# Pooled attention with a token mixer: dividing by the row sums when a batch is loaded, not per head pair

## The chip, the cores and the metric

The kernel runs on one core of one Trainium2 chip. A core has five engines with instruction queues of their own: TensorE (PE, with its weight loads shown apart as PEld), VectorE (DVE), ScalarE (ACT), GpSimd (POOL) and SyncE (SP), whose queue issues nearly all DMAs here. The metric is the device time of one execution in microseconds (us).

## The reference, cut to what matters

```python
# attention: q, k, v are (8 batches, 8 heads, 1152, 64); two neighbouring rows of q are averaged
scores = scale * np.matmul(q_pool, k.transpose(0, 1, 3, 2))          # (8, 8, 576, 1152)
scores = scores - np.max(scores, axis=-1, keepdims=True)
attn = np.exp(scores)
attn = attn / (np.sum(attn, axis=-1, keepdims=True) + 1e-09)
x = np.matmul(attn, v)                                               # heads side by side: (8, 576, 512)
# token mixer
theta = x @ w_theta
zr, zi = x * np.cos(theta), x * np.sin(theta)
u = x + w_tok_r @ zr + w_tok_i @ zi                                  # over tokens, per batch
out = u + np.maximum(u @ w_ch, 0.0)
```

The four weight matrices arrive as 64-bit floats, as pairs of 32-bit words, and are turned into 32-bit floats on the chip.

## The kernel before, in words

There are two phases. The attention phase runs over 32 pairs of heads (`i`, four pairs to a batch). The token phase runs over 8 batches (`b`).

**Order.** Every piece of work is registered with a position (`at` in the first phase, `at2` in the second), the list is sorted, and each engine then executes its own instructions strictly in that order. A pair is 18 positions long (two halves `u` of the query rows, nine key tiles `kt` each). The tables at the head of the file (`PLAN`, `W_AT`, `MAX_AT`, `TOK_AT` and so on) hold the positions. An instruction that waits holds up everything behind it on its engine, and on SP a DMA that waits holds up every later DMA.

**One pair.** `prep_t`, `prep_hi` and `prep_lo` transpose keys and queries on PE, round them on ACT (`hi`) and take the remainder on DVE (`lo`). `maxpass` and `max_tail` find row maxima: PE writes scores to PSUM, DVE reduces them (`mx`, lines 287, 306 and 307). `escore` computes each score tile with eight matmuls and ACT takes the exponential (`pc`, line 349). `ssum` adds the exponentials on POOL (`ss`, line 358). `av` multiplies them with the values (line 367) into `xu`. `norm_sum` finishes the row sums on PE and ACT adds epsilon (`sm`). PSUM is cut into four slots, used in turn by all of these. Twice in a pair, at positions 10.35 and 19.27, a `burst` stands: the transposes for a later pair, the rounding, and an `av`. In the second burst (`tail_prep`) DVE reads the slots with `mx` L306 and L307, ACT then writes `hi`, DVE writes `lo`, and only then can PE use the slot again. In the first one ACT's small copies (`tail`, then `mT` of L319) stand behind DVE's `lo`, and PE's `norm_sum` stands behind `mT`.

**Division before.** For each pair the four rows of sums go to DRAM (`norm_spread`), come back spread over 128 partitions (`norm_load`), are inverted on DVE (`norm_recip`, 128x9), go to DRAM again (`norm_save`), come back copied to 64 partitions each (`norm_bcast`, two DMAs), and DVE multiplies the pair's output by them (`norm_out`, L429, 128x576). `norm_store` then writes the pair to `xd[b]`.

**Weights.** A generator (`weights`) makes 18 jobs of some fifteen steps; nine steps stand in each pair, at the positions `W_AT`: four just ahead of the first burst, three just ahead of the second. A job fetches a slab (`raw`, one buffer), and `narrow` makes 32-bit floats with six operations on DVE (L500, L503, L505, L507, L511, L515), one on ACT (L502) and two on POOL.

**Token phase.** `xload` brings a batch into `xT` (two buffers), `xhi` (ACT) and `xlo` split it, `theta` multiplies (PE), `chain` makes sine and cosine and the products in eight steps on ACT, DVE and, last, POOL (`zlo`, L771), `token_mix` and `channel` multiply. `xlo` runs on DVE for batch 0 and on POOL for the others (L704). Batch 0 is loaded while the last pairs of the first phase still run.

Of the kernel before, what the change touches and what calls it, by code (L numbers as in the profile page):

```python
# [9 lines left out]
F32 = mybir.dt.float32  # L10
# [27 lines left out]
    "norm_spread": 29.0,  # L38
    "norm_load": 29.426,
    "norm_recip": 37.5,  # L40
    "norm_save": 37.6,
    "norm_bcast": 37.7,
    "norm_out": 46.5,
    "norm_store": 46.6,
}
# [6 lines left out]
CYC = 56  # L52
PLAN2 = {'wload': 12.0, 'xload': -64.6, 'xhi': -51.7, 'uadd0': 15.0, 'uadd1': 31.4}
THETA_AT = (-42.4, -33.8, -25.1, -15.4, -9.2)
THETA0_AT = (-70, -60, -50, -40, -30)
CHAIN0_AT = (0.5, 2, 4, 8, 13, 18, 26, 28)
X0_AT = 563
X1_AT = -4
CHAIN_AT = (4.4, 2.4, 6.3, 5.7, 10.3, 8.7, 2.8, 4.5)
# [19 lines left out]
def pooled_attention_moe_kernel(  # L79
# [48 lines left out]
    wcd = [dram.tile([ND, P, DM], F32, name=f"wcd{i}") for i in range(2)]  # L128
    xd = [dram.tile([DM, SQ], F32, name=f"xd{b}") for b in range(B)]

    def bank(kind, name):
# [22 lines left out]
    xTs = []  # L154

    def xload(b):
        xT = xTs[b % 2]
        bst[b] = {"xT": xT}
        xv = xd[b].rearrange("(c p) s -> p c s", p=P)
        nc.sync.dma_start(xT[:, :, 0:SQ], xv)  # L160
        nc.sync.dma_start(xT[:, :, SQ : 5 * P], xv[:, :, 4 * P : SQ])

    with ExitStack() as p1:
# [196 lines left out]
        def av(i, u):  # L360
            st = state[i]
            if u == 0:
                st["xu"] = nrm.tile([P, 2, HALF], F32, tag="xu", name=f"xu{i}", bufs=3)
            pa = bank2("e", f"pa{i}_{u}")
            for kt in range(KT):
                for h, hs in enumerate(HEADS):
                    nc.tensor.matmul(  # L367
                        pa[hs, 0, 0:HALF],
                        st["vn"][:, h, kt, :],
                        st["pc"][u, kt][:, h, :],  # L370
                        start=(kt == 0),
                        stop=(kt == KT - 1),
                    )
            nc.scalar.copy(st["xu"][:, u, :], pa[:, 0, 0:HALF])
# [19 lines left out]
        def norm_spread(i):  # L394
            st = state[i]
            rdi = st["rd"] = dram.tile([4, HALF], F32, tag="rd", name=f"rd{i}", bufs=2)
            nc.sync.dma_start(rdi, st["sm"].rearrange("(n r) c -> n r c", r=32)[:, 0, :])

        def norm_load(i):
            st = state[i]  # L400
            rc = st["rc"] = sml.tile([P, SQ * 2 // P], F32, tag="rc", name=f"rc{i}")
            rdv = st["rd"].rearrange("n c -> (n c)").rearrange("(p j) -> p j", p=P)
            nc.sync.dma_start(rc, rdv)

        def norm_recip(i):
            rc = state[i]["rc"]
            nc.vector.reciprocal(rc, rc)

        def norm_save(i):
            st = state[i]  # L410
            rdo = st["ro"] = dram.tile([4, HALF], F32, tag="ro", name=f"ro{i}", bufs=2)
            nc.sync.dma_start(
                rdo.rearrange("n c -> (n c)").rearrange("(p j) -> p j", p=P), st["rc"]
            )

        def norm_bcast(i):
            st = state[i]
            dn = st["dn"] = nrm.tile([P, 2, HALF], F32, tag="dn", name=f"dn{i}")
            for h in range(2):
                nc.sync.dma_start(  # L420
                    dn[h * D : (h + 1) * D].rearrange("a u c -> a (u c)"),
                    st["ro"].rearrange("(h u) c -> h (u c)", h=2)[h : h + 1, :].broadcast_to(
                        [D, SQ]
                    ),
                )

        def norm_out(i):
            st = state[i]
            nc.vector.tensor_tensor(st["xu"], st["xu"], st["dn"], ALU.mult)  # L429

# [32 lines left out]
        def norm_store(i):  # L463
# [4 lines left out]
            )  # L468
            del state[i]

        def weights():
# [17 lines left out]
            def narrow(raw, ws, R, n, g):  # L489
# [9 lines left out]
                mk = ws[0:R, 0:n]  # L499
                nc.vector.tensor_scalar(lo, lo, 8, None, ALU.logical_shift_right)  # L500
                yield
                nc.scalar.activation(tl, lo, AF.Copy, scale=2.0**-44)  # L502
                nc.vector.tensor_scalar(f, hi, 0x7FFFFFFF, None, ALU.bitwise_and)  # L503
                yield
                nc.vector.tensor_scalar(mk, f.bitcast(F32), TINY, None, ALU.max)  # L505
                yield
# [114 lines left out]
        def plan(i):  # L621
# [24 lines left out]
            for n, fn in (  # L646
                ("norm_spread", norm_spread),
                ("norm_load", norm_load),
                ("norm_recip", norm_recip),
                ("norm_save", norm_save),  # L650
                ("norm_bcast", norm_bcast),
                ("norm_out", norm_out),
                ("norm_store", norm_store),
# [6 lines left out]
        pw = ExitStack()  # L660
        wgen = weights()
        at(X0_AT, 11, early)
        for i in range(NPAIR):
            for pos in W_FIRST if i == 0 else W_AT if i < W_END else W_LAST:
# [4 lines left out]
    with ExitStack() as p2:  # L669
# [221 lines left out]
        for b in range(B):  # L891
            base = CYC * b
            if b > 0:
                at2(base + PLAN2["xload"] if b > 1 else X1_AT, xload, b)
            xat = PLAN2["xhi"] if b else THETA0_AT[0] - 4
# [63 lines left out]
```

## Time and profile before

| | |
|---|---|
| median of three runs | 1422.18 us (1422.18 to 1427.7) |
| the profiled execution, first to last instruction | 1422.1 us |
| busy, PE / PEld | 1343.2 us (94%) / 1094.5 us (77%) |
| busy, DVE / ACT / POOL | 858.6 us (60%) / 724.5 us (51%) / 913.0 us (64%) |
| attention phase, token phase | up to about 920 us, and from there |
| mean granted clock of PE | 0.989 of full |

Busy shares are means over both phases, so the share of one stage has to be read from that stage. A gap in PE is what costs time here; the other engines matter where PE waits for them.

### The profile page before, as it was taken

How to read it: one execution, taken by the hardware profiler on the slowest of the kernel's cores; microseconds unless marked ns; L12 is line 12 of the kernel's file. 1: busy time of each engine (PE TensorE's matmuls, PEld its weight loads, DVE VectorE, ACT ScalarE, POOL GpSimd, SP SyncE). 2: the span in 40 equal slices, each digit the busy share in tenths (PEclk: the TensorE clock that was granted, in tenths of full speed). 3: DMA queues.
4: the chain of work that ended last, by engine and by line, in shares of the span. 5: the costliest groups of instructions: out<-in, count | busy, mean ns of one | idle time of the engine just before them, and what ended most of it. 6: DMA issues, size and time to landing. Idle time of an engine off the chain costs nothing.

```text
span 1422.1 us, 29902 instructions
## 1 busy us (share of the span) xinstructions
PE 1343.2 (94%) x12178; PEld 1094.5 (77%) x12178; DVE 858.6 (60%) x1140; ACT 724.5 (51%) x1254; POOL 913.0 (64%) x671
## 2 busy tenths in 40 slices
PE   5999899999999999999998999989999999999998
PEld 4767677767766776767676776679999999999998
DVE  5866676667677767766675667165353543536342
ACT  2555455646555565556564655564344544445431
POOL 2789788988897998879987898842323313232210
PEclk9999999999999999999999999989999999999999
DMA  5224333424342353324333431321111111111111
GB/s 126 74 75 128 82 101 93 110 83 125 94 116 79 98 140 89 91 83 126 99 94 85 118 85 49 98 100 38 34 38 34 52 57 34 38 34 42 30 32 36
DMA packets 130906, 111.66 MB, mean 79 GB/s; under 512 B 95040, under 2 KB 95424, under 8 KB 130768
## 3 DMA queue, kind: packets, MB, share of 16 engines
q1 hardware_dynamic: 130592, 109.28, 28.0%
q8 instruction: 96, 1.57, 0.5%
q0 software_dynamic: 176, 0.46, 0.1%
q14 instruction: 42, 0.34, 0.1%
HBM read 88.29 MB, written 21.27 MB: 77 GB/s over the span
## 4 chain that ended last, share of the span: by engine, by line
PE 64%; DVE 18%; ACT 6%; DMA 5%; issue 3%; POOL 3%; SPq 1%; ACTq 0%; POOLq 0%; DVEq 0%
PE pe L346 15%; PE py L796 13%; PE pa L367 11%; PE pth L724 7%; DVE mx L287 6%; PE pr L835 6%; PE pm L280 3%; PE pt L240 3%; DMA kn<-in_k_dram 2%; PE pmt L383 2%; POOL ss L358 2%; DVE lo L267 2%; DVE ws L505 1%; DVE wf L503 1%; DVE mx L306 1%
## 5 line engine op out<-in xcount | busy, mean ns | idle before, releaser
L358 POOL TENSOR_TENSOR ss<-ss,pc 128x576 f32<-128x576 f32 x384 | 561.0, 1461 | 110.8 <-ACT pc L349 88.7
L287 DVE TENSOR_REDUCE mx<-pm 128x2 f32<-128x768 f32 x384 | 344.5, 952 | 138.2 <-PE pm L280 138.0
L349 ACT ACTIVATE pc<-pe 128x576 f32<-128x576 f32 x576 | 365.0, 652 | 90.0 <-PE pe L346 71.6
L367 PE MATMUL pa<-pc,vn 128*64 128x288 f32 x2304 | 293.5, 409 | 1.1 <-PE pmt L317 1.0
L771 POOL TENSOR_TENSOR Z<-ab,Z 128x512 fp32r<-128x512 f32 x40 | 52.3, 1308 | 315.1 <-ACT Z L767 315.1
L796 PE MATMUL py<-wtk,Z 128*128 128x288 f32 x1728 | 244.7, 299 | 6.9 <-DVE r L741 6.9
L367 PEld LDWEIGHTS pa<-pc,vn 128*64 128x64 f32 x2304 | 162.3, 137 | 109.5 <-ACT pc L349 3.2
L796 PEld LDWEIGHTS py<-wtk,Z 128*128 128x128 f32 x1728 | 235.7, 191 | 8.7 <-DVE r L741 7.5
L346 PE MATMUL pe<-hi 64*128 64x288 f32 x1152 | 206.4, 353 | 19.2 <-DVE lo L267 17.5
L346 PEld LDWEIGHTS pe<-hi 64*128 64x128 f32 x1152 | 110.6, 187 | 87.5 <-issue 28.8
L346 PE MATMUL pe<-lo,hi 64*128 64x288 f32 x1152 | 173.3, 296 | 0.0
L346 PE MATMUL pe<-hi,lo 64*128 64x288 f32 x1152 | 173.0, 295 | 0.0
L346 PE MATMUL pe<-nmr,oner 64*128 64x288 f32 x1152 | 172.3, 294 | 0.0
L280 PE MATMUL pm<-hi 64*128 64x384 f32 x768 | 138.2, 357 | 10.8 <-DVE mx L306 6.0
L256 ACT CAST hi<-pt 128x768 fp32r<-128x768 f32 x64 | 56.2, 878 | 117.8 <-DVE mx L307 103.1
L346 PEld LDWEIGHTS pe<-lo,hi 64*128 64x128 f32 x1152 | 112.1, 190 | 0.0
L346 PEld LDWEIGHTS pe<-hi,lo 64*128 64x128 f32 x1152 | 111.4, 189 | 0.0
L346 PEld LDWEIGHTS pe<-nmr,oner 64*128 64x128 f32 x1152 | 111.3, 188 | 0.0
L267 DVE TENSOR_TENSOR lo<-pt,hi 128x768 fp32r<-128x768 f32 x64 | 67.6, 1056 | 65.1 <-ACT hi L256 65.1
L835 PEld LDWEIGHTS pr<-us,wch 128*128 128x128 f32 x768 | 104.5, 188 | 1.8
L835 PE MATMUL pr<-us,wch 128*128 128x288 f32 x768 | 105.8, 295 | 0.0
L358 POOL TENSOR_TENSOR ss<-pc,pc 128x576 f32<-128x576 f32 x64 | 95.3, 1489 | 3.5 <-ACT pc L349 3.4
(103 smaller groups left out, 1653.7 us busy)
## 6 DMA issues: line engine op xcount, KB each, us to landing
qn<-in_q_dram SPq DMA_DIRECT2D x32, 576.0 KB
kn<-in_k_dram SPq DMA_DIRECT2D x64, 288.0 KB
vn<-in_v_dram SPq DMA_DIRECT2D x32, 576.0 KB
dn<-ro SPq DMA_DIRECT2D x64, 144.0 KB
xd<-xu SPq DMA_DIRECT2D x32, 288.0 KB
xT<-xd SPq DMA_DIRECT2D x8, 1152.0 KB
out_dram<-on SPq DMA_DIRECT2D x23, 192.0 KB
out_dram<-on SPq DMA_DIRECT2D x23, 128.0 KB
```

Source lines behind the costliest of these rows:

```text
L256: nc.scalar.copy(hi, src)
L267: nc.vector.tensor_tensor(lo, src, hi.bitcast(F32), ALU.subtract)
L280: nc.tensor.matmul(pm[:, h, 0:W], hi[hs, Q0 + j * P : Q0 + (j + 1) * P], hi[hs, K0[3 * g] : K0[3 * g] + W], start=True, stop=True,)
L287: nc.vector.tensor_reduce(mx[:, j : j + 5 : 4, g : g + 1], pm[:, :, 0:W], AX.X, ALU.max)
L346: nc.tensor.matmul(pe[:, h, 0:HALF], w[hs], x[hs], start=(n == 0), stop=(n == 3))
L349: nc.scalar.activation(pcs[u, kt], pe[:, :, 0:HALF], AF.Exp, scale=SC)
L358: nc.gpsimd.tensor_tensor(st["ss", u], first, st["pc"][u, kt], ALU.add)
L367: nc.tensor.matmul(pa[hs, 0, 0:HALF], st["vn"][:, h, kt, :], st["pc"][u, kt][:, h, :], start=(kt == 0), stop=(kt == KT - 1),)
L724: nc.tensor.matmul(th, xs[:, c, j * P : (j + 1) * P], ws[:, c], start=(n == 0), stop=(n == 11))
L771: engine("zlo", b).tensor_tensor(Z[1], t, Z[0].bitcast(F32), ALU.subtract)
L796: nc.tensor.matmul(st["py", c, u][:, 0:HALF], Z[zi][:, c * P : (c + 1) * P], wtk[wi][:, kw, u * HALF : (u + 1) * HALF], start=(i == 0 and ...
L835: nc.tensor.matmul(pr[u][:, 0:HALF], wch[wi][:, c, e * P : (e + 1) * P], st["us", ui][:, c, u * HALF : (u + 1) * HALF], start=(n == 0), st ...
```

## The change

Per pair, `norm_load`, `norm_recip`, `norm_save`, `norm_bcast` and `norm_out` are gone; `norm_spread` writes the sums of the pair to a DRAM tile of its batch (`sd[b]`), and `norm_store` writes the undivided output, 26 positions earlier. Per batch, `rload`, `recip` (128x36) and `rsave` make the inverses. `dload` brings them copied over 64 partitions, for each quarter `c` of the batch, into one of three buffers, and `xscale` multiplies `xT` in place, with two operations a quarter (128x576 and 128x64): on DVE for batch 0, on POOL for the other seven. `xload` of batches 1 to 7 stands earlier in the order. In `narrow` the shift and the sign mask on DVE are replaced: ACT's copy reads the low word as it is, and a second ACT operation takes the absolute value of the high word. The generator has one step less per job.

```diff
     "norm_spread": 29.0,
-    "norm_load": 29.426,
-    "norm_recip": 37.5,
-    "norm_save": 37.6,
-    "norm_bcast": 37.7,
-    "norm_out": 46.5,
-    "norm_store": 46.6,
+    "norm_store": 20.5,
...
-PLAN2 = {'wload': 12.0, 'xload': -64.6, 'xhi': -51.7, 'uadd0': 15.0, 'uadd1': 31.4}
+PLAN2 = {'wload': 12.0, 'xload': -79.5, 'xhi': -51.7, 'uadd0': 15.0, 'uadd1': 31.4}
...
-X1_AT = -4
+X0_DN = (0.1, 0.2, 0.3, 5.3)
+X0_SC = (5.0, 5.5, 6.0, 9.0)
+R_AT = (16.0, 24.5, 24.6)
+DN_AT = (-83.9, -83.8, -83.7, -69.3)
+SC_AT = (-69.4, -69.3, -60.0, -59.9)
...
+    def rload(b):
+        bst[b] = {}
+        rc = bst[b]["rc"] = dnp.tile([P, H * SQ // P], F32, tag="rc", name=f"rc{b}", bufs=2)
+        nc.sync.dma_start(rc, flat(sd[b]))
+    def recip(b):
+        rc = bst[b]["rc"]
+        nc.vector.reciprocal(rc, rc)
+    def rsave(b):
+        nc.sync.dma_start(flat(rd[b]), bst[b]["rc"])
+    def dload(b, c):
+        dn = bst[b]["dn", c] = dnp.tile([P, SQ], F32, tag="dn", name=f"dn{b}_{c}", bufs=3)
+        for h in range(2):
+            src = rd[b].rearrange("(h u) c -> h (u c)", u=2)[2 * c + h : 2 * c + h + 1, :]
+            nc.sync.dma_start(dn[h * D : (h + 1) * D], src.broadcast_to([D, SQ]))
+    def xscale(b, c, eng):
+        xT, dn = bst[b]["xT"], bst[b]["dn", c]
+        eng.tensor_tensor(xT[:, c, 0:SQ], xT[:, c, 0:SQ], dn, ALU.mult)
+        eng.tensor_tensor(
+            xT[:, c, SQ : 5 * P], xT[:, c, SQ : 5 * P], dn[:, 4 * P : SQ], ALU.mult
+        )
...
-                st["xu"] = nrm.tile([P, 2, HALF], F32, tag="xu", name=f"xu{i}", bufs=3)
+                st["xu"] = nrm.tile([P, 2, HALF], F32, tag="xu", name=f"xu{i}", bufs=2)
...
         def norm_spread(i):
+            b, hp = divmod(i, NP)
             nc.sync.dma_start(
+                sd[b][4 * hp : 4 * hp + 4], state[i]["sm"].rearrange("(n r) c -> n r c", r=32)[:, 0, :]
             )
-        def norm_out(i):
-            st = state[i]
-            nc.vector.tensor_tensor(st["xu"], st["xu"], st["dn"], ALU.mult)
...
-                nc.vector.tensor_scalar(lo, lo, 8, None, ALU.logical_shift_right)
-                yield
-                nc.scalar.activation(tl, lo, AF.Copy, scale=2.0**-44)
-                nc.vector.tensor_scalar(f, hi, 0x7FFFFFFF, None, ALU.bitwise_and)
-                yield
-                nc.vector.tensor_scalar(mk, f.bitcast(F32), TINY, None, ALU.max)
+                nc.scalar.activation(tl, lo, AF.Copy, scale=2.0**-52)
+                nc.scalar.activation(mk, hi.bitcast(F32), AF.Abs)
+                yield
+                nc.vector.tensor_scalar(mk, mk, TINY, None, ALU.max)
                 yield
...
+        for b in range(B - 1):
+            for n, fn in enumerate((rload, recip, rsave)):
+                at(NU * (4 * b + 4) + R_AT[n], 12, fn, b)
         at(X0_AT, 11, early)
+        for c in range(ND):
+            at(X0_AT + X0_DN[c], 13, dload, 0, c)
+            at(X0_AT + X0_SC[c], 14, xscale, 0, c, nc.vector)
...
-                at2(base + PLAN2["xload"] if b > 1 else X1_AT, xload, b)
+                if b == B - 1:
+                    for n, fn in enumerate((rload, recip, rsave)):
+                        at2(-60 + 10 * n, fn, b)
+                at2(base + PLAN2["xload"], xload, b)
+                for c in range(ND):
+                    at2(base + DN_AT[c], dload, b, c)
+                    at2(base + SC_AT[c], xscale, b, c, nc.gpsimd)
```

The line numbers of the changed file are higher by 30 in the attention phase (L306 becomes L336, L358 becomes L388); the weight operations of DVE are L502, L504, L508 and L512 there.

**DVE ahead of the second burst of pair 15.** `mx17<-px17` is the reduce with which that burst begins on DVE, L500 to L505 are weight steps, `lo` is the remainder that frees the slot. Before:

```order
L287 TENSOR_REDUCE mx17_6369<-pm17_12_6463 128x2
L500 TENSOR_SCALAR raw_6282<-raw_6282 128x512
L503 TENSOR_SCALAR wf_6468<-raw_6282 128x512
L505 TENSOR_SCALAR ws_6281<-wf_6468 128x512
L306 TENSOR_REDUCE mx17_6369<-px17_6508 128x2
L307 TENSOR_REDUCE mx17_6369<-pt0_18_6501 128x1
L267 TENSOR_TENSOR lo18_6500<-pt0_18_6501,hi18_6499 128x768
```

The same place now:

```order
L317 TENSOR_REDUCE mx17_6260<-pm17_11_6340 128x2
L317 TENSOR_REDUCE mx17_6260<-pm17_12_6355 128x2
L336 TENSOR_REDUCE mx17_6260<-px17_6398 128x2
L337 TENSOR_REDUCE mx17_6260<-pt0_18_6391 128x1
L297 TENSOR_TENSOR lo18_6390<-pt0_18_6391,hi18_6389 128x768
```

And now ahead of the second burst of pair 11 (before, no weight step of DVE stood there, but two remainders of finished weights, L151):

```order
L317 TENSOR_REDUCE mx13_4739<-pm13_12_4834 128x2
L502 TENSOR_SCALAR ws_4653<-ws_4653 128x576
L504 TENSOR_SCALAR wf_4760<-ws_4653 128x576
L508 SCALAR_TENSOR_TENSOR wf_4760<-raw_4654,wf_4760 128x576
L336 TENSOR_REDUCE mx13_4739<-px13_4877 128x2
```

With fewer steps in a job the steps fall on other positions, so each burst has another set ahead of it than before.

**SP in one pair.** `mT` is the row of maxima, `kn` and `vn` are keys and values, `sm` and `rd` the sums, `raw` a slab of weights. Before:

```order
L215 DMA vn10_4023<-in_v_dram 128x2x576
L397 DMA rd8_4025<-sm8_4001 4x288
L403 DMA rc8_4033<-rd8_4025 128x9
L412 DMA ro8_4197<-rc8_4033 128x9
L420 DMA dn8_4200<-ro8_4197 64x576 x2
L191 DMA qn13_4324<-in_q_dram 96x2x768
L545 DMA wcd0_80<-hl_4154 128x512
```

Now:

```order
L245 DMA vn10_3971<-in_v_dram 128x2x576
L426 DMA sd2_92<-sm8_3951 4x288
L542 DMA wcd0_80<-hl_3888 128x512
L542 DMA wcd1_81<-hl_3889 128x512
L485 DMA raw_4089<-in_moe_w_tok_r_dram 64x1152 x2
L466 DMA xd2_84<-xu9_3922 128x576
L221 DMA qn13_4268<-in_q_dram 96x2x768
```

Four DMAs of the pair, three of which wait for the one before them, no longer stand ahead of the fetch of weights and of the next `qn`.

**POOL where the token phase begins.** `Z1` with index 6, 3, 7 and 8 are the last remainders of batch 0 (`zlo`), `xl1` the remainder of batch 1. Before:

```order
L771 TENSOR_TENSOR Z10_6_12826<-ti_12775,Z00_6_12825 128x512
L771 TENSOR_TENSOR Z10_3_12839<-ab_12815,Z00_3_12838 128x512
L771 TENSOR_TENSOR Z10_7_12842<-ti_12817,Z00_7_12841 128x512
L771 TENSOR_TENSOR Z10_8_12848<-ab_12834,Z00_8_12847 128x512
L704 TENSOR_TENSOR xl1_12894<-xT1_12629,xh1_12893 128x640 x4
```

Now:

```order
L769 TENSOR_TENSOR Z10_6_12568<-ti_12508,Z00_6_12567 128x512
L181 TENSOR_TENSOR xT1_12358<-xT1_12358,dn1_0_12548 128x576
L182 TENSOR_TENSOR xT1_12358<-xT1_12358,dn1_0_12548 128x64
L181 TENSOR_TENSOR xT1_12358<-xT1_12358,dn1_1_12551 128x576
L182 TENSOR_TENSOR xT1_12358<-xT1_12358,dn1_1_12551 128x64
L769 TENSOR_TENSOR Z10_3_12583<-ab_12557,Z00_3_12582 128x512
L769 TENSOR_TENSOR Z10_7_12586<-ti_12559,Z00_7_12585 128x512
L181 TENSOR_TENSOR xT1_12358<-xT1_12358,dn1_2_12554 128x576
L182 TENSOR_TENSOR xT1_12358<-xT1_12358,dn1_2_12554 128x64
L181 TENSOR_TENSOR xT1_12358<-xT1_12358,dn1_3_12592 128x576
L182 TENSOR_TENSOR xT1_12358<-xT1_12358,dn1_3_12592 128x64
L769 TENSOR_TENSOR Z10_8_12599<-ab_12578,Z00_8_12598 128x512
```

The four scalings of batch 1 now stand between the remainders of batch 0, and `xl1` follows the last of them. For the later batches the order is the same.

## Rows read from the trace of the kernel before

**Rows 1.** Busy time by stage (--windows): stretch, length, PE, PEld, DVE, ACT, POOL, clock, DMA.
```profile
35.00:905.00 870.00, 823.80 (x8631) 611.92 (x8631) 601.05 (x710) 486.98 (x854) 747.53 (x539) 0.99 0.36 98
985.00:1400.00 415.00, 412.76 (x2842) 392.19 (x2842) 190.85 (x329) 184.35 (x311) 117.34 (x85) 1.00 0.14 40
```

**Rows 2.** Waits of PE from 35 to 905: total us, times, longest us.
```profile
PE pe L346 <- DVE lo L267: 17.5, 12, 1.6
PE pmt L383 <- ACT mT L319: 12.1, 10, 2.4
PE pm L280 <- DVE mx L306: 6.0, 4, 2.6
```

**Rows 3.** Groups by line, DVE from 35 to 905; ACT's weight copy, whole span.
```profile
L429 DVE TENSOR_TENSOR xu<-xu,dn 128x576 f32<-128x576 f32 x30 | 34.1, 1136 | 6.6 <-DMA dn<-ro 6.6
...
L503 DVE TENSOR_SCALAR wf<-raw 128x512 uint32<-128x512 uint32 (+2 forms) x18 | 22.8, 1265 | 0.0
...
L500 DVE TENSOR_SCALAR raw<-raw 128x512 uint32<-128x512 uint32 (+2 forms) x18 | 19.0, 1054 | 27.2 <-POOL ss L358 10.5 <-DMA raw<-in_moe_w_tok_i_dram 7.0 <-DMA raw<-in_moe_w_ch_dram 6.7
...
L515 DVE TENSOR_SCALAR raw<-wf 128x512 uint32<-128x512 uint32 (+2 forms) x18 | 11.6, 647 | 0.3
...
L502 ACT ACTIVATE raw<-raw 128x512 f32<-128x512 uint32 (+2 forms) x18 | 12.8, 712 | 13.2 <-DVE raw L500 13.2
```

**Rows 4.** Timeline, second burst of pair 12: start, length, engine, instruction, [idle before].
```profile
394.20 1.22 DVE L507 TENSOR_SCALAR wf<-ws 128x576 uint32<-128x576 uint32 x1
...
395.45 2.39 DVE L511 SCALAR_TENSOR_TENSOR wf<-raw,wf 128x576 uint32<-128x576 uint32 x1
...
397.88 1.55 DVE L515 TENSOR_SCALAR raw<-wf 128x576 uint32<-128x576 uint32 x1
...
399.35 1.21 DVE L306 TENSOR_REDUCE mx<-px 128x2 f32<-128x1024 f32 x1
...
402.63 0.40 PE L346 MATMUL pe<-hi 64*128 64x288 f32 x2 [1.45 <-DVE lo L267]
```

**Rows 5.** Timeline, second burst of pair 8, SP and DVE.
```profile
283.38 0.33 SPq L403 DMA_DIRECT2D rc<-rd  x1
283.82 0.37 SPq L486 DMA_DIRECT2D raw<-in_moe_w_ch_dram  x1
...
287.24 0.85 DVE L500 TENSOR_SCALAR raw<-raw 128x512 uint32<-128x512 uint32 x1 [5.13 <-DMA raw<-in_moe_w_ch_dram]
```

**Rows 6.** Timeline, first burst of pair 14, ACT and PE.
```profile
443.05 0.42 ACT L263 CAST tail<-pt 64x64 fp32r<-64x64 f32 x2 [4.99 <-DVE lo L267]
...
443.80 0.69 PE L383 MATMUL pmt<-ss,ones 128*32 128x288 f32 x8 [2.35 <-ACT mT L319]
```

**Rows 7.** Busy time in stretches at half clock, columns as in rows 1.
```profile
149.17:156.00 6.83, 5.70 (x46) 5.70 (x48) 4.67 (x7) 4.16 (x8) 4.80 (x4) 0.50 0.36 90
...
766.99:770.40 3.41, 3.16 (x24) 3.17 (x26) 2.65 (x6) 1.76 (x4) 2.41 (x2) 0.50 0.07 20
```

**Rows 8.** Timeline, end of the attention phase, DVE and POOL.
```profile
899.32 1.94 DVE L429 TENSOR_TENSOR xu<-xu,dn 128x576 f32<-128x576 f32 x1 [6.56 <-DMA dn<-ro]
...
900.60 1.95 POOL L358 TENSOR_TENSOR ss<-ss,pc 128x576 f32<-128x576 f32 x1
...
911.44 8.83 POOL L358 TENSOR_TENSOR ss<-ss,pc 128x576 f32<-128x576 f32 x6
```

**Rows 9.** Timeline, start of the token phase, DVE, POOL and PE.
```profile
935.09 0.75 DVE L429 TENSOR_TENSOR xu<-xu,dn 128x576 f32<-128x576 f32 x1
...
955.13 6.14 POOL L704 TENSOR_TENSOR xl<-xT,xh 128x640 fp32r<-128x640 f32 x4
...
964.05 1.08 PE L724 MATMUL pth<-wth,xl 128*128 128x512 f32 x4
```

**Rows 10.** Token phase, batch 1: POOL's timeline; DMA after the load of batch 2.
```profile
1011.30 1.28 POOL L771 TENSOR_TENSOR Z<-ab,Z 128x512 fp32r<-128x512 f32 x1 [4.23 <-ACT Z L767]
...
991.50:995.00 3.50, 3.50 (x23) 3.21 (x22) 1.83 (x4) 2.54 (x5) 1.72 (x2) 1.00 0.00 0
```

More of the change, by code (lines that the diff above doesn't have):

```diff
@@ L129, in pooled_attention_moe_kernel @@
     xd = [dram.tile([DM, SQ], F32, name=f"xd{b}") for b in range(B)]
+    sd = [dram.tile([2 * H, HALF], F32, name=f"sd{b}") for b in range(B)]
+    rd = [dram.tile([2 * H, HALF], F32, name=f"rd{b}") for b in range(B)]
+    dnp = ctx.enter_context(tc.tile_pool(name="dnp", bufs=1))
     def bank(kind, name):
@@ L154, in pooled_attention_moe_kernel, with flat @@
     xTs = []
+    def flat(d):
+        return d.rearrange("n c -> (n c)").rearrange("(p j) -> p j", p=P)
+    def rload(b):
[18 more added lines that the diff above has]
+        )
     def xload(b):
         xT = xTs[b % 2]
-        bst[b] = {"xT": xT}
+        bst[b]["xT"] = xT
         xv = xd[b].rearrange("(c p) s -> p c s", p=P)
@@ L394, in norm_spread @@
         def norm_spread(i):
-            st = state[i]
[L396 to L411, printed above, removed]
+            b, hp = divmod(i, NP)
             nc.sync.dma_start(
-                rdo.rearrange("n c -> (n c)").rearrange("(p j) -> p j", p=P), st["rc"]
+                sd[b][4 * hp : 4 * hp + 4], state[i]["sm"].rearrange("(n r) c -> n r c", r=32)[:, 0, :]
             )
[L416 to L425, printed above, removed]
-        def norm_out(i):
-            st = state[i]
-            nc.vector.tensor_tensor(st["xu"], st["xu"], st["dn"], ALU.mult)
+            del state[i]
         def burst(i, u):
@@ L468, in norm_store @@
             )
-            del state[i]
         def weights():
@@ L647, in plan @@
                 ("norm_spread", norm_spread),
[L648 to L652, printed above, removed]
                 ("norm_store", norm_store),
```

## The prediction, made before the changed kernel ran

> **What bounds the kernel now.** I read the stages first [rows 1]. In the token phase PE is busy for 412.8 of 415 us, so nothing is to be won there, and much could be lost. In the attention phase from 35 to 905 us it is busy for 823.8 of 870, so 46.2 us of PE are idle: that is the purse. The waits of PE say who holds it [rows 2]. Two rows belong to the second burst of a pair: the score matmuls wait for DVE's remainder (17.5 us, 12 times), and the maximum matmuls wait for the reduce of L306 (6.0 us, 4 times). Together 23.5 us, half of the idle time. The third row belongs to the first burst (12.1 us, 10 times). Three rows thus hold 35.6 of the 46.2 us.
>
> The timeline then shows why DVE is late in the second burst [rows 4]. The reduce L306 starts at 399.35, and right ahead of it stand three weight operations of 1.22, 2.39 and 1.55 us. They have nothing to do with the burst, but the order puts them there. PE then stands for 1.45 us. Going through the bursts in the order of DVE, eight have three weight operations ahead of them; at 1.45 us each they hold 11.6 us. Four more bursts have a DVE that waits for the fetch of a slab [rows 5]: it stands 5.13 us in L500, because SP issued the fetch only at 283.82, just after the load of L403, which had waited for the DMA before it. The four cost PE what is left of the 23.5, 11.9 us, or 3 us each.
>
> In the first burst [rows 6] ACT stands 4.99 us until DVE's remainder is through, which itself is behind three or four weight operations, and PE stands 2.35 us for ACT's copy.
>
> There is a second price. PE's granted clock falls to 0.50, the lower of its two levels (1.2 of 2.4 GHz), in four stretches of the attention phase, the first of 6.83 us and the others of 3.41, 17.1 us together [rows 7]. Three of the four come right behind a burst that waited for a slab, the fourth behind a wait in a first burst. At half clock half of the time is lost, so 17.1 / 2 = 8.5 us.
>
> **The change part by part.** *Weight steps on DVE.* L500 (18 times 1.054 us) and L503 (18 times 1.265) go: 41.8 us of DVE [rows 3]. DVE is no bound by its sum, so this pays only where the operations stood ahead of a burst. Placing the shorter jobs on the same positions, the second bursts now have: three weight operations in three pairs (0, 11 and 19); two behind ACT's two conversions in three pairs (3, 14 and 22), where DVE cannot start before ACT has done both, 2 x 0.71 us, so that the sum is like three; two short ones or one in six or seven; none in the others. By the 1.4 us of today's triples, and 0.5 less for the two triples that end in L515, which is shorter by 0.6 us [rows 3], the six cost 0.9 + 1.4 + 0.9 + 3 x 1.4 = 7.4 us, the rest about 0.9. So 23.5 becomes 8.3: **-15.2 us**. Bounds: 0 left, and 18 left if every pair behind ACT pays like the slab waits do (3 us).
>
> *The slab waits.* With L403 gone from SP, the fetch is issued right behind the write of the sums, about 3 to 4 us earlier. They are contained in the 15.2. One is left to be watched, in pair 17, where ACT's conversion stands two positions behind its fetch: now ACT waits there and not DVE, and I put 0.5 us of the 0.9 on it.
>
> *First bursts.* After the change three pairs have four weight operations there, the last of them the short one, one has ACT's conversions and three, two have the conversions and two, and in two ACT waits for POOL's last weight step. The one with conversions and three gets the 2.35 us of rows 6; the other seven I put at 0.7, between nothing and today's mean of 12.1 / 10 = 1.2: 7.2 us against 12.1, **-4.9 us**, bounds -12 and +3.
>
> *L429 and L407 in the attention phase.* 30 times 1.136 us of DVE [rows 3]. L429 stands behind the remainder in its burst, and DVE has waits for PE afterwards; what it delays are some maxima: **-1 us**, bounds -4 and 0.
>
> *Clock.* With most slab waits gone at least three of the four falls have no cause left; new ones can come behind the first bursts that stay. **-5 us** of the 8.5, bounds -8.5 and +2.
>
> *ACT's second operation.* 18 on ACT; the trace has none of this form, the nearest is the copy of the low word with the same stride, 0.71 us [rows 3]: 12.8 us. ACT is busy for 487 of 870 us, and PE has up to four slots of scores ahead, which is the cover. Bounds 0 and 12.8; I take **+1.5**, near the lower end, because the wait on DVE that ACT had here (13.2 us, same row) goes at the same time.
>
> *End of the attention phase.* POOL's running sums are back to back to the end (six in 8.83 us, [rows 8]), and PE's last row sums wait for them. There DVE will multiply batch 0, four times 128x576 and four times 128x64. When DVE's L429 overlapped POOL's sum, both took 1.95 us; POOL's alone takes 8.83 / 6 = 1.47, so it lost about 0.5 us. Four times 0.5, four small ones at 0.1, less the one L429 that goes: **+2.0 us**, bounds 0 and 5. The Trainium skill ("SBUF — State Buffer", "Who interferes with whom") says that a DVE instruction with two SBUF inputs and a POOL instruction that reads SBUF exclude each other for a whole instruction; with the uncontended 0.75 us of L429 [rows 9] as the time locked out, POOL would lose 4 x 0.75 and, at an estimate of 0.2 us, 4 small ones, less 0.75: 3.0 us, and the sum would end one higher. The one overlap in the rows cost POOL less than the whole instruction, so the trace agrees only in the direction, and I keep 2.0.
>
> *Start of the token phase.* DVE is the chain here, and L429 (0.75 us, [rows 9]) goes while a reciprocal comes: **-0.5 us**. The two pairs of scalings of batch 1 now stand in POOL's order between the remainders of batch 0. A scaling is a 128x576 of 1.47 us (as POOL's sum) and a 128x64, which the trace does not have; between nothing and 1.28 us, POOL's time for 512 columns [rows 10], I take 0.4, as most of the time of these operations goes with the columns. So 1.87 each and 7.5 in all, bounds 5.9 and 11. POOL starts the next `xl` at 955.13 and ends it at 961.3 [rows 9]; it was idle for a little ahead of these remainders, for which I take off 1.5, between nothing and the 4.23 of the same place a batch later [rows 10]. With the scalings it ends at 961.3 + 7.5 - 1.5 = 967.3. PE wants the first quarter at 964.05 and the last one 0.8 us later [rows 9], all half a us earlier by the term before: it waits 2.9 us. **+2.9 us**, bounds 0 and 7. The load of batch 1 is asked for later than before, behind the inverse of batch 7; as POOL comes to it only after the third chain, I take nothing for that.
>
> *Later batches.* Scalings 7.5 us a batch, 45 us in six batches on POOL, which is busy for 117 of 415 us [rows 1]. The narrowest place is ahead of the last remainder of a batch, where POOL has 4.23 us of idle time [rows 10] for two scalings of 3.7. **0 us**, covered by that idle time; if it were too short, `xl` would come later, and its use is several us behind. Uncovered they would cost up to 45.
>
> *SP.* Per pair four DMAs go; per batch ten come in. The two of the attention phase stand behind the fetches and loads of their pair, and those of the token phase wait for one of the three buffers where SP's next work, the stores of a batch, is not due yet. **0 us**.
>
> The profiled execution spans 1422.1 us, 0.1 less than the median. Sum: 1422.1 - 15.2 - 4.9 - 1 - 5 + 1.5 + 2.0 - 0.5 + 2.9 = 1401.9. I say 1402 us.
>
> **Rivals.** *A, the relief goes further.* With DVE less busy all second bursts run without a wait (-23.5), the first ones nearly so (-10), and the clock stays up (-8); the 5.9 us added elsewhere remain: 1422.1 - 41.5 + 5.9 = 1386.5. For it: 41.8 + 34.1 = 76 us less on DVE [rows 3]. Against: six second bursts still have as much ahead of them.
>
> *B, the stall moves to ACT.* The two conversions stand ahead of exponentials and of the rounding, and DVE's next weight step now waits for ACT. Then only the slab waits (11.9) and three falls of the clock ((6.83 + 2 x 3.41) / 2 = 6.8) are won, and half of ACT's 12.8 us is paid, beside the 4.4 us net of the two phases' meeting: 1422.1 - 18.7 + 6.4 + 4.4 = 1414. For it: DVE and ACT are coupled more tightly. Against: ACT is busy for 56% of the phase [rows 1].
>
> *C, nothing is won.* The positions stay and the jobs are shorter, so other steps fall ahead of the bursts, and they hold PE up as long as the old ones: 1422 to 1425. Against: there are fewer operations of any kind ahead of them.
>
> *D, slower.* POOL in the token phase: a batch's scalings wait for its load, and they stand ahead of the remainders that PE's token mixing needs. From the point where the load comes about 15 us later than today's, it is later than the idle time of POOL in rows 10 (1007.1 to 1011.3), and each further us is paid in seven batches; 5 us beyond it cost 35, and the time is about 1437. Against: the load of batch 2 has ended by 991.5 [rows 10].
>
> **How the numbers follow.** Forecast 0.60, A 0.15, B 0.14, C 0.07, D 0.04. The range takes in A's end and B's: 1385 to 1415. A measurement of this kernel can tell about 0.5%, that is 7 us, from no change; faster than 1415 are the forecast, A and most of B: 0.85; the rest of B and C: 0.11 the same; D: 0.04 slower.
>
> **What would show it.** In the profile after: PE's waits for `lo` and for L306's successor between 35 and 900 down from 23.5 us to about 8, the wait for `mT` to about 7; no DVE instruction that stands 5 us for a slab; one or no stretch at half clock before 900; PE waiting some 2 us for `xl` of batch 1, and PE as full as now from there on. Wrong it would be if PE's waits for ACT's exponentials grew by more than 5 us, if POOL's scalings held up the token phase, or if DVE's waits for ACT put the old 1.4 us back in most bursts.

## The result, and the profile after

The changed kernel takes 1407.88 us (median of four runs, 1407.65 to 1409.69) against 1422.51 us for the kernel before on the same chip: ratio 0.9896, 95% interval 0.9874 to 0.9918, so about 1.0% faster. The forecast was 1402 us in a range of 1385 to 1415: faster, as said, but the gain is 6 us short of it. The profiled execution went from 1422.1 to 1405.9 us.

The result has two halves, cut at PE's last row sums. They end at 921.5 us before and at 895.3 after, so the attention phase won 26.2 us; from there to the end it is 500.6 us before and 510.6 after, so 10.0 us were given back. First the busy time by stage, as in [rows 1].

```profile
35.00:890.00 855.00, 829.42 (x8765) 614.00 (x8765) 540.41 (x631) 504.03 (x884) 748.76 (x548) 1.00 0.34 91
890.00:905.00 15.00, 11.22 (x51) 8.08 (x52) 5.61 (x7) 3.30 (x6) 2.98 (x2) 0.66 0.01 2
985.00:1384.00 399.00, 393.49 (x2715) 372.80 (x2714) 182.83 (x307) 174.85 (x294) 156.81 (x125) 1.00 0.18 53
```

PE now lacks 25.6 us of the attention phase's 855, where it lacked 46.2 of 870, and the granted clock is 1.00 there: all four falls of [rows 7] are gone. In the token phase it lacks 5.5 us of 399, where it lacked 2.2 of 415. PE's waits from 35 to 890 us, as in [rows 2]:

```profile
PE pmt L413 <- ACT mT L349: 8.6, 8, 2.3
PE pe L376 <- DVE lo L297: 4.8, 4, 1.5
PE pm L310 <- DVE mx L317: 3.3, 5, 0.9
PE pe L376 <- ACT pc L379: 2.5, 5, 0.7
```

The second burst's row fell from 17.5 to 4.8 us, and L306's (L336 now) is no longer in the list. The last two rows are what took a part of it back. PE's waits from 893 us on:

```profile
PE py L794 <- DVE r L739: 6.9, 2, 4.7
PE pend L413 <- POOL ss L388: 5.2, 1, 5.2
PE po L856 <- ACT on L873: 4.8, 7, 0.8
PE pth L722 <- POOL xl L702: 2.5, 2, 1.5
```

Before, the second and the third row read as follows, and the fourth was not there:

```profile
PE pend L383 <- POOL ss L358: 1.7, 1, 1.7
PE po L858 <- ACT on L875: 1.5, 7, 0.5
```

So the end of the attention phase, batch 1's `xl` and the copied output tile of each batch are the three places that give back. During the wait for POOL's sums and right behind that for `xl` the clock falls as well (stretches, columns as in [rows 1]):

```profile
889.98:900.22 10.24, 6.45 (x26) 4.14 (x27) 3.39 (x3) 1.74 (x3) 3.00 (x2) 0.50 0.01 2
917.28:927.52 10.24, 5.72 (x24) 5.72 (x25) 10.10 (x11) 6.44 (x12) 7.51 (x6) 0.50 0.29 97
944.59:948.00 3.41, 3.41 (x15) 3.33 (x15) 2.31 (x4) 1.73 (x3) 0.00 (x0) 0.50 0.02 5
```

The middle stretch was there before (10.24 us from 941.07); the other two are new. Last, the weight steps of the changed kernel, answering to [rows 3]: ACT's two and the first of DVE's.

```profile
L499 ACT ACTIVATE raw<-raw 128x512 f32<-128x512 uint32 (+2 forms) x18 | 12.8, 709 | 5.2 <-DMA raw<-in_moe_w_tok_r_dram 2.3 <-DMA raw<-in_moe_w_tok_i_dram 2.0 <-DMA raw<-in_moe_w_theta_dram 1.0
L500 ACT ACTIVATE ws<-raw 128x512 f32<-128x512 f32 (+2 forms) x18 | 12.5, 696 | 0.0
...
L502 DVE TENSOR_SCALAR ws<-ws 128x512 f32<-128x512 f32 (+2 forms) x18 | 16.6, 923 | 17.0 <-ACT ws L500 17.0
```

The wait for a slab shrank from 27.2 us on DVE (10.5 of them stand as waits for POOL, in two places where SP had issued the fetch only 3 to 5 us before) to 5.2 on ACT. New is DVE's own: 17.0 us in which it stands for ACT's absolute value.

### The profile page after: what moved, and what is told of

Same layout as the page of the kernel before. It is cut to its first block, busy times and chain, and to the rows that moved or that the text cites. A ratio compares the mean times of both kernels' runs of the same rounds, so it can differ in the third digit from the quotient of the medians.

```text
span 1405.9 us, 29815 instructions
## 1 busy us (share of the span) xinstructions
PE 1341.1 (95%) x12178; PEld 1090.6 (78%) x12178; DVE 804.1 (57%) x1056; ACT 735.5 (52%) x1272; POOL 958.8 (68%) x727
## 4 chain that ended last, share of the span: by engine, by line
PE 72%; DVE 12%; ACT 7%; POOL 4%; issue 3%; DMA 2%; SPq 0%; ACTq 0%; POOLq 0%; DVEq 0%
PE pe L376 19%; PE pa L397 14%; PE py L794 12%; PE pth L722 7%; PE pr L833 6%; PE pm L310 4%; PE pt L270 3%; DVE mx L317 3%; PE pmt L413 2%; POOL ss L388 2%; ACT pc L379 2%; DVE wf L504 1%; DVE wf L508 1%; PE pxn L710 1%; DVE lo L297 1%
## 5 line engine op out<-in xcount | busy, mean ns | idle before, releaser
L388 POOL TENSOR_TENSOR ss<-ss,pc 128x576 f32<-128x576 f32 x384 | 553.7, 1442 | 95.1 <-ACT pc L379 72.4
L317 DVE TENSOR_REDUCE mx<-pm 128x2 f32<-128x768 f32 x384 | 344.4, 952 | 175.4 <-PE pm L310 175.3
L388 POOL TENSOR_TENSOR ss<-pc,pc 128x576 f32<-128x576 f32 x64 | 91.9, 1436 | 3.4 <-ACT pc L379 3.4
```

Source lines behind the costliest of these rows:

```text
L317: nc.vector.tensor_reduce(mx[:, j : j + 5 : 4, g : g + 1], pm[:, :, 0:W], AX.X, ALU.max)
L388: nc.gpsimd.tensor_tensor(st["ss", u], first, st["pc"][u, kt], ALU.add)
```

## The experiments

Ratios are to the kernel before on the same chip, with 95% intervals.

### Which part won it

One part alone each: the four-operation conversion in the kernel before, and the moved division with the six-operation conversion.

```
e1_weights, in the kernel before:        e2_division, in the changed kernel:
-  DVE: lo >> 8                          -  ACT: tl = copy(lo) * 2^-52
-  ACT: tl = copy(lo) * 2^-44            -  ACT: mk = abs(hi)
-  DVE: f = hi & 0x7FFFFFFF              +  DVE: lo >> 8
+  ACT: tl = copy(lo) * 2^-52            +  ACT: tl = copy(lo) * 2^-44
+  ACT: mk = abs(hi)                     +  DVE: f = hi & 0x7FFFFFFF
   DVE: mk = max(mk, TINY)                  DVE: mk = max(f, TINY)
```

> The weight conversion with four operations, in the kernel before: the division by the row sums stays in the attention phase. Theory S (the one behind the prediction): the four slab waits and the falls of the clock behind them come from the loads of the division that stand on SP ahead of the fetches, so both stay here: PE's idle time in the attention phase falls from 45.5 us by the triples and first bursts only, to about 34, one fall of the clock goes, and the time is about 1422.5 - 10.5 - 1.7 = 1410 us. Rival W: the slab waits cost PE only because DVE stood in them; now ACT stands there and PE's scores ahead cover it, so this part alone does all that the attention phase won (22.4 + 8.5 us), and without the 14.5 us that the division costs later: 1422.5 - 30.9 = 1392, to 1396 us.

> The division moved to the token phase, the weight conversion with its six operations on DVE. Theory S: SP fetches the slabs earlier, so the four slab waits (11.9 us) and three of the four falls of the clock (6.8 us) go, and what comes later costs 14.5 us (3.5 at the end of the attention phase, 11 after it): 1422.5 - 18.7 - 1 + 14.5 = 1417 us; no DVE instruction stands 5 us for a slab. Rival W: the weight steps alone made the gain; the waits in the attention phase and its falls of the clock stay as in the kernel before, and the time is 1422.5 - 1 to 2 + 14.5 = 1435 us.

The weights alone: 1411.47 us, ratio 0.9916 (0.989 to 0.9941), as theory S said. The division alone: 1426.39 us, ratio 1.0014 (1.0001 to 1.0028), between the two: S promised too much. PE's busy time from 35 to 890 us, first of the weights alone, then of the division alone:

```profile
35.00:890.00 855.00, 821.33 (x8636) 610.29 (x8637) 565.34 (x674) 498.50 (x872) 745.89 (x539) 0.99 0.37 99
```

```profile
35.00:890.00 855.00, 814.94 (x8551) 603.00 (x8550) 568.77 (x657) 481.40 (x845) 732.30 (x535) 0.99 0.32 87
```

PE lacks 33.7 and 40.1 us in these, 46.0 before and 25.6 with both: the two parts win 12.3 and 5.9 apart and 20.4 together. (The profiled executions of the two lie 2 us off their medians, the first below and the second above, so a difference between traces carries that much.) What joins the parts, by the rows, is the wait for a slab. The weights alone (ACT's first operation) and the division alone (DVE's):

```profile
L500 ACT ACTIVATE raw<-raw 128x512 f32<-128x512 uint32 (+2 forms) x18 | 12.8, 709 | 16.1 <-DMA raw<-in_moe_w_tok_r_dram 7.0 <-DMA raw<-in_moe_w_tok_i_dram 4.7 <-DMA raw<-in_moe_w_theta_dram 4.3
```

```profile
L499 DVE TENSOR_SCALAR raw<-raw 128x512 uint32<-128x512 uint32 (+2 forms) x18 | 18.0, 998 | 20.7 <-DMA raw<-in_moe_w_tok_r_dram 10.7 <-DMA raw<-in_moe_w_ch_dram 4.3 <-DMA raw<-in_moe_w_tok_i_dram 3.5
```

27.2 us before, 16.1, 20.7 (one of them 5.9 us long, where S expected none of 5), and 5.2 with both. Neither an earlier fetch alone nor ACT as the reader alone removes it. Three falls of the clock stay in each of the two kernels ahead of 890 us, none with both. From the last row sums to the end the weights alone take 501.3 us and the division alone 512.2: what is given back belongs to the division. On top of the weights it won 11.0 us up to that point and lost 9.3 after it.

### The end of the attention phase

In the changed kernel DVE's scalings of batch 0 run beside POOL's last sums (DVE, then POOL, then PE's last row sums; the answer to [rows 8]):

```profile
879.46 0.88 DVE L181 TENSOR_TENSOR xT<-xT,dn 128x576 f32<-128x576 f32 x1 [26.67 <-DMA dn<-rd]
880.27 1.45 DVE L182 TENSOR_TENSOR xT<-xT,dn 128x64 f32<-128x64 f32 x1
881.64 0.75 DVE L181 TENSOR_TENSOR xT<-xT,dn 128x576 f32<-128x576 f32 x1
```

```profile
881.71 11.35 POOL L388 TENSOR_TENSOR ss<-ss,pc 128x576 f32<-128x576 f32 x6
```

```profile
893.11 0.70 PE L413 MATMUL pend<-ss,ones 128*32 128x288 f32 x3 [5.16 <-POOL ss L388]
```

Six sums take 11.35 us, not 8.83. The 128x64 operation is a ninth of the other's size and takes twice as long. Three of POOL's sums one by one, begun beside a pair of scalings, with nothing beside it, and beside `xl` of batch 0 on DVE:

```profile
883.74 1.94 POOL L388 TENSOR_TENSOR ss<-ss,pc 128x576 f32<-128x576 f32 x1
887.77 1.41 POOL L388 TENSOR_TENSOR ss<-ss,pc 128x576 f32<-128x576 f32 x1
889.26 1.86 POOL L388 TENSOR_TENSOR ss<-ss,pc 128x576 f32<-128x576 f32 x1
```

Each of the four pairs of scalings costs POOL about 0.53 us (1.94 to 1.96 for 1.41), 2.1 in all, and `xl` costs it 0.45 twice. A pair costs POOL no more than one 128x576 operation did in [rows 8] (1.95 us there): the small operation waits, and POOL hardly pays for it.

```
e3_scale0_early:   -X0_AT = 563                  +X0_AT = 545
e10_last_sums_pe:  as e3_scale0_early, and in the last pair's second half
                   -if kt == 0 or kt >= 8        +if kt == 0 or kt >= 5   # running sums on POOL
                   norm_sum reads tiles 5 to 8 by matmul (8 alone before),
                   and POOL's sum last, not first (in all pairs)
```

> The changed kernel with the load and the scaling of batch 0 18 positions (a pair) earlier, so that DVE's eight multiplications no longer stand beside POOL's last running sums. Theory: PE's wait for the last running sum falls from 5.16 to 2 us or less, and the 10.24 us at half clock right behind it (from 890 us) go or get shorter, which is worth 3 to 5 us more: 1407.9 - 3.2 - 3.5 = about 1401 us. Rival: POOL is behind anyway in the last two pairs (78 of 90 us busy), what it loses earlier it carries on to the end, the wait stays at about 5 us and the time at 1408 us.

> The changed kernel with the early scaling of batch 0 (as in the run before), and in the last pair the last three running sums of its second half left out on POOL: PE's row sums read those three tiles themselves (12 more matmuls of 128x288). Theory: PE's wait for POOL's last running sum falls from 3.2 us to under 1, and as the fall of the clock at 891 us follows that wait, it goes with it: 1406 - 2.5 - 3 = about 1401 us. Rival: the clock falls there whatever the wait, because little work is left for PE between the two phases: the fall stays, and the time is about 1404 us.

Early scaling: 1406.14 us, ratio 0.9881 (0.9864 to 0.9897); that the time is better than the changed kernel's is not told apart by these intervals, but the trace moved. PE's wait went from 5.16 to 3.16 us, not to the 2 that I had expected, and the fall that begins in it from 10.24 to 6.83. The two operations without and with a neighbour, in one trace (POOL ended a sum at 858.64 and was idle up to 860.99):

```profile
857.29 1.43 DVE L182 TENSOR_TENSOR xT<-xT,dn 128x64 f32<-128x64 f32 x1
858.65 0.75 DVE L181 TENSOR_TENSOR xT<-xT,dn 128x576 f32<-128x576 f32 x1
859.32 0.21 DVE L182 TENSOR_TENSOR xT<-xT,dn 128x64 f32<-128x64 f32 x1
```

0.21 us beside an idle POOL, 1.43 beside a running sum: it stands until POOL's operation is through. With the last three sums on PE the time is 1401.77 us, ratio 0.9846 (0.9824 to 0.9867), and PE does not wait for POOL at all. POOL ends at 888.28 us there, ahead of PE's row sums at 889.78, so the fewer sums end this wait, and the turned order of the matmuls was not needed for it. The stretch from 890 to 905 us, with the early scaling and then with the sums on PE too:

```profile
890.00:905.00 15.00, 12.98 (x60) 9.53 (x61) 7.45 (x11) 5.34 (x8) 1.30 (x1) 0.77 0.01 2
```

```profile
890.00:905.00 15.00, 14.36 (x87) 10.59 (x80) 8.83 (x15) 9.46 (x16) 0.00 (x0) 1.00 0.06 22
```

Clock 0.66 in the changed kernel, 0.77, 1.00: the fall goes with the wait. The last run also gives PE twelve matmuls more in this place, so by itself it does not rule out the rival (little work for PE there anyway). Other kernels do: the one before, with PE's work as in the changed kernel and a wait of 1.7 us, has no fall between 905 and 941 us; the weights alone, with a wait of 2.40, have 3.41 us at half clock behind it (from 907.27), and the division alone, with 3.80, has 6.83 (from 914.30).

### The token phase

```
                     SC_AT (third and fourth scaling)    engine, batches 2 to 7
changed kernel       -60.0,  -59.9                       POOL
e4_scalings_apart    -54.0,  -53.9                       POOL
e7_scalings_early    -61.2,  -61.15                      POOL
e8_scalings_dve      -61.2,  -61.15                      DVE
```

> The changed kernel with the third and fourth scaling of batches 1 to 7 on POOL six positions later, behind the last chain of the batch before and not beside it. Theory: POOL's multiplications slow the DVE operations of that chain, so ACT's copy of the first output tile comes late; with them apart PE's waits for that copy fall from 5.5 us to about 2.5, and its wait for xl of batch 1 from 2.5 to about 1: about 1403.5 us. Rival: the copy is late for the order on ACT alone, the waits stay, and xh of the next batch now waits for POOL: 1408 to 1412 us.

> The changed kernel with the third and fourth scaling of batches 2 to 7 on POOL ahead of the remainders of Z3 and Z7, right behind the first two, and so not beside the last chain of the batch before. Theory: DVE's wait-free run of that chain comes back (ACT's idle time for ab of the last chain from 1.41 us to about 0.8, as the run with the scalings moved later had it), and xh no longer waits for POOL either: PE's waits for the copied output tile fall from 5.5 us to 2.5 or less, about 1404.5 us. Rival: the scalings slow the chain before it and make Z3 and Z7 late by 4 us, PE's token mixing waits for them: 1408 us or more.

> The same places, but the scalings of batches 2 to 7 on DVE and not on POOL (batch 1 stays on POOL). DVE is busy for 183 of 399 us there, and a pair takes about 1 us on it. Theory: nothing of the token phase waits for POOL's scalings any more and DVE's chains are late by 1 to 4 us where they have room: PE's waits for the copied output tile fall from 5.5 us to 2.5, about 1404.5 us. Rival: DVE is the chain that makes Z, each microsecond ahead of it is paid: 4 us a batch, 1425 us at most.

(The 5.5 us in these count small waits that the view above leaves out.) ACT at the end of a batch, in the changed kernel, then with the scalings later, then earlier:

```profile
991.33 0.62 ACT L765 CAST Z<-ab 128x512 fp32r<-128x512 f32 x1 [1.41 <-DVE ab L759]
991.85 0.58 ACT L873 COPY on<-po 128x512 f32<-128x512 f32 x1
```

```profile
992.87 0.62 ACT L765 CAST Z<-ab 128x512 fp32r<-128x512 f32 x1 [0.83 <-DVE ab L759]
...
996.53 0.72 ACT L698 CAST xh<-xT 128x640 fp32r<-128x640 f32 x1 [1.31 <-POOL xT L182]
997.17 0.58 ACT L873 COPY on<-po 128x512 f32<-128x512 f32 x1
```

```profile
989.81 0.62 ACT L765 CAST Z<-ab 128x512 fp32r<-128x512 f32 x1 [0.83 <-DVE ab L759]
```

With POOL's scalings out of the last chain, ACT waits 0.83 us for `ab` in both, as it did in this place before the change (at 1010.60); with them beside it, 1.41, and so at the same place of six batches (1.40 or 1.41; 0.83 in all six with the scalings earlier). The multiplication on DVE that ACT waits for, in the changed kernel and then with the scalings earlier:

```profile
990.02 1.28 DVE L759 TENSOR_TENSOR ab<-xn,ab 128x512 f32<-128x512 f32 x1 [1.50 <-ACT ab L756]
```

```profile
989.08 0.69 DVE L759 TENSOR_TENSOR ab<-xn,ab 128x512 f32<-128x512 f32 x1 [1.49 <-ACT ab L756]
```

That half of the theory holds. Later is still worse (1414.65 us, ratio 0.9934, 0.9918 to 0.9951): `xh` stands in ACT's queue ahead of the copy of the next output tile and now waits for POOL, and PE's waits for the copy go to 10.5 us. Earlier pays neither: they fall to 1.3 us and the profiled span from 1405.9 to 1402.8. Its time of 1406.63 us (ratio 0.9883, 0.986 to 0.9905) cannot be told from the changed kernel's by itself. With the scalings on DVE it is 1415.51 us (0.9942, 0.9922 to 0.9963): worse, against my theory, but less than the rival's most. PE now waits for DVE's `uT`:

```profile
PE po L856 <- DVE uT L846: 9.9, 6, 1.7
```

### ACT's second operation

```
e5_abs_twice:    ACT: tl = copy(lo);  ACT: mk = abs(hi);  +ACT: mk = abs(hi)
e12_abs_on_dve:  ACT: tl = copy(lo);  -ACT: mk = abs(hi)  +DVE: f = hi & 0x7FFFFFFF
e15_copy_later:  ACT: mk = abs(hi);  yield;  DVE: max;  ACT: tl = copy(lo)
```

> The changed kernel with ACT's second operation of each weight slab issued twice: 18 times 0.70 us, 12.5 us more on ACT in the attention phase, in the same places. Theory: PE has scores ahead of ACT, so it is covered but for 1 to 2 us: 1409 to 1410 us (the changed kernel: 1407.9). Rival: ACT's operations stand right ahead of exponentials and of the row of maxima and are paid one for one in half of the pairs: PE's waits for ACT's pc and mT grow by 5 us or more, and the time is 1413 to 1420 us.

> The changed kernel with the absolute value of a slab on DVE again (as a bitwise and, the form that the kernel before had, 1.27 us) and not on ACT (0.70 us), in the same step. Theory M: both engines pay for what stands ahead of a burst, ACT about 0.74 us for each us (9.3 for 12.5 in the run with the operation twice), DVE about 0.55 (the weight part alone won some 14 us net of ACT's price, for 41.8 us of DVE): 18 x (1.27 x 0.55 - 0.70 x 0.74) = +3 us, 1411 us. Rival: ACT's cover is enough for one such operation and not for two, as the prediction had it; then nothing is won on ACT, and DVE's 22.8 us cost 12: 1420 us.

> The changed kernel with ACT's copy of the low word one step later than its absolute value (its only reader, POOL's multiplication, comes four steps behind), so that the two no longer stand together in one place. Theory: the 1.4 us in one place is what PE's cover does not hold; in two places of 0.7 us PE's waits for lo, mT and pc in the attention phase fall from 15.9 us by 3 to 4: 1404 us. Rival: it is the amount of ACT work that counts, and other bursts now have a copy ahead of them: 1407 to 1410 us.

Twice: 1417.2 us, ratio 0.9954 (0.994 to 0.9967), about 8 us worse for 12.5 us of ACT. My theory that PE's cover holds it fell. The rival had the time right and the place only in part: PE's wait for `mT` grew from 8.6 to 10.9 us and that for `lo` from 4.8 to 8.1, and those for `pc` did not grow. The absolute value on DVE: 1409.47 us, 0.9884 (0.9862 to 0.9907), the changed kernel's time within the intervals; the rival's 1420 is out, and theory M's 3 us are not seen. Copy later: 1402.7 us, 0.9842 (0.9821 to 0.9863), as expected and a little more; PE's waits for `lo`, `mT` and `pc` fell from 15.9 to 12.9 us, as expected too, but the reason that I had put down isn't what the trace shows. One first burst, the changed kernel and then the later copy:

```profile
395.38 0.69 ACT L499 ACTIVATE raw<-raw 128x512 f32<-128x512 uint32 x1
395.96 0.67 ACT L500 ACTIVATE ws<-raw 128x512 f32<-128x512 f32 x1
...
396.73 1.16 DVE L502 TENSOR_SCALAR ws<-ws 128x512 f32<-128x512 f32 x1 [1.37 <-ACT ws L500]
...
403.10 0.69 PE L413 MATMUL pmt<-ss,ones 128*32 128x288 f32 x8 [2.26 <-ACT mT L349]
```

```profile
394.03 0.67 ACT L499 ACTIVATE ws<-raw 128x512 f32<-128x512 f32 x1
394.61 0.67 ACT L502 ACTIVATE raw<-raw 128x512 f32<-128x512 uint32 x1
...
394.81 0.43 DVE L501 TENSOR_SCALAR ws<-ws 128x512 f32<-128x512 f32 x1 [0.81 <-POOL ss L388]
```

The two operations still stand side by side here. What changed is that the one DVE reads comes first, ends 0.7 us earlier, and DVE's step starts right behind it: DVE stands 0.81 us (put down to POOL here), not 1.37, and PE's wait in this burst falls from 2.26 to 0.97. That DVE's operation takes 0.43 us here and not 1.16 helps too, but belongs to this place: over all 18 its mean is no shorter (1143 against 923 ns). Over the phase DVE's wait ahead of this step is 26.7 us with the operation twice, 17.0 in the changed kernel and 10.9 with the later copy, and the times stand in the same order. That fits ACT's operations costing mainly as DVE's wait; three kernels in one order do not prove it. How much of the gain (5 us by the medians, 8 by the ratios) is the order and how much the step between them these runs do not part.

### Together

```
e13_both_repairs  = e10_last_sums_pe + e7_scalings_early
e14_three_repairs = e13_both_repairs + e15_copy_later
```

> The two repairs together: early scaling of batch 0 with the last three sums on PE, and the third and fourth scaling of batches 2 to 7 ahead of the remainders of Z3 and Z7. Theory: they lie in different phases and add: 1401.8 - 2.3 to 3 = 1399 us, no fall of the clock between 880 and 905 us, po waits of 3.2 us. Rival: what the token phase wins is in waits that do not sum (output tiles have slack): 1401 to 1402 us.

> The two repairs and the later copy together. Theory: the copy's gain lies in the attention phase, the repairs' at its end and in the token phase, so they add: 0.9816 + 0.9842 - 0.9896 = 0.976 of the kernel before, about 1389 us at its 1422.5. Rival: POOL is the next bound of the attention phase (it is busy for 88% of it), so that of the 5 to 7 us of the copy only a part is left: 1394 us or more.

1398.73 us, ratio 0.9816 (0.9791 to 0.9841): the time agrees with the two adding up, though the part of the earlier scalings is too small to be told by time alone. With the later copy 1393.95 us, ratio 0.979 (0.9774 to 0.9805), about 2.1% faster than the kernel before: it beats both kernels. The time is the rival's 1394, and the theory's ratio of 0.976 lies outside the interval. How much of the copy's gain is left stays open: a half by the ratios (0.0026 of 0.0054), nearly all by the medians (4.8 of 5.2 us), and the intervals are as wide as these differences. That POOL is what bounds it I have not tested.

## Why the prediction was right, and where it was off

| term | predicted, us | measured in the traces, us |
|---|---|---|
| second bursts | -15.2 | -18.7 by the two rows; 2.8 come back as waits for L317 |
| first bursts | -4.9 | -3.5 |
| waits for `kn` (5.6 before, not in the sum) | 0 | -5.6 |
| ACT's second operation | +1.5 | +2.1 as waits for `pc`; the rest is in the rows above |
| clock, attention phase | -5 | -8.5 |
| end of the attention phase | +2.0 | +3.5, and about 2.5 for the fall that begins there |
| `xl` of batch 1 | +2.9 | +2.5, and 1.7 for the fall behind it |
| start of the token phase | -0.5 | 0 (6.9 us of waits for `r`, as before) |
| later batches | 0 | +3.3 |

The waits for `kn`, in the kernel before from 35 to 905 us (in the changed kernel no such row is left from 35 to 890):

```profile
PE pt L240 <- DMA kn<-in_k_dram: 5.6, 7, 1.2
```

*What held.* The purse was the idle time of PE in the attention phase, and the two bursts held it: no DVE instruction of the weights stands 5 us for a slab any more, and no fall of the clock is left before 889. The forecast would have been 4 us too high there (22.6 us net to the last row sums, measured 26.2). PE's wait for `xl` was 2.5 us where I had 2.9. That the sum as a whole came within 4 us of the profiled 1405.9 is partly luck: the attention phase won 3.6 us more than forecast, 5.6 of it in waits for `kn` that were not in the sum, and the rest of the kernel gave back 7.6 us more (10.0 where I had 2.4), so that the two errors partly cancel.

*The step that failed: "Later batches. 0 us, covered by that idle time".* The idle time of [rows 10] is indeed there: it shrank from 4.23 to 0.55 us, and PE waits for no `xl` after that of batch 1. But I asked only whether POOL has room, not who else is slowed: POOL's scalings make DVE's last chain later (ACT's wait for `ab` from 0.83 to 1.41), the output tile's copy stands behind it in ACT's queue, and PE paid 3.3 us. The run with the scalings earlier took the row from 4.8 to 1.3 us. This was none of my rivals (D looked for the load), but it is one of the signs of being wrong that the prediction names: POOL's scalings held up the token phase.

*"End of the attention phase +2.0".* For the scalings the size was nearly right, and two other things were missing. I had 2.4 us for the four pairs before L429 was taken off, and POOL lost 2.1 to them. `xl` of batch 0 ran beside the last two sums too, for 0.9 us, and about 0.7 us come without any scaling: with the weights alone the wait is 2.40 us and not 1.7. The division alone, where one `xl` runs beside a sum, has 3.80. The rule of the Trainium skill ("SBUF — State Buffer", "Who interferes with whom"), by which such operations exclude each other whole, gave 3.0. The 0.21 against 1.43 us of the small operation on DVE agree with the rule; the price worked out from it, 0.95 us a pair, does not agree with the 0.53 that POOL lost. The fall of the clock in the wait was not in the sum: 4.96 us of it lie behind the last row sums, at half clock.

*"SP 0 us".* The queue was not free of cost: the load of batch 0 was issued at 869.22, right behind the store of pair 30, DVE stood 26.67 us for it, and so the scalings fell on POOL's last sums. A pair earlier they did not.

*"The slab waits. With L403 gone from SP, ..." and ACT's +1.5.* The slab waits went, but not by SP alone, as the division alone shows (20.7 of 27.2 us stay). And work on ACT in this place is dearer than I said: one more such operation per slab, 18 in all, costs some 8 us. What the second one itself costs no run shows by itself; with its work back on DVE the time is the same. Rival B had the right wait (DVE for ACT, 17.0 us) and came out 8 us too high: of the bursts it counted the slab waits alone, 11.9 us, where the two rows fell by 18.7.

## What to carry to other kernels

Cost a moved operation at three engines: its own, the one whose operations it slows beside it (here DVE for POOL and POOL for DVE), and the one whose queue holds the next step behind that. When work is split between two engines, issue first the part that the other one waits for. Ahead of a phase's end, look at which engine finishes last there, and keep new work away from it.

## What the runs showed of the hardware

- A DVE multiplication with two SBUF inputs beside a POOL addition takes 1.43 us at 128x64 and 0.21 alone, so about 1.2 us of it is waiting. The POOL addition lost 0.53 us (1.94 for 1.41) beside a 128x576 and a 128x64 of these.
- PE's granted clock fell to 0.50 (1.2 of 2.4 GHz) while PE waited for POOL's last sums or right behind that wait: for 10.24 us with a wait of 5.16, 6.83 with 3.80 and with 3.16, 3.41 with 2.40, not at all there with 1.7 and without a wait. These are single executions, one of each kernel, and the length does not follow the wait alone: with 4.6 us it was 6.83 with the absolute value on DVE and 10.24 with the later copy.
- A POOL scaling of 128x576 takes 1.52 us and one of 128x64 0.55 in the token phase, 2.07 together where I had 1.87.
